# Moving about half of the shifted copies of the powers from VectorE to GpSimd in an attention-plus-MLP kernel

## The chip, the cores and the metric

The kernel runs on one core of a Trainium2 chip. A core has five engines that run side by side, each through its own instructions in a fixed order: TensorE (PE in the profile, its weight loads PEld), VectorE (DVE), ScalarE (ACT), GpSimd (POOL) and SyncE (SP, which here only issues transfers). They wait for one another through semaphores. The metric is the time of one execution on the device in microseconds, the median of several runs; lower is better.

## The reference, cut to what matters

The input x has 2048 rows of 640. Branch A is softmax attention with 32 heads of width 20, branch B a dense layer with the Mish activation; a sigmoid gate per row mixes them.

```python
def _A_ref(x, wqkv, wo):
    H = 32; Dh = D // H                                   # D = 640, Dh = 20
    qkv = (x @ wqkv).reshape(B, S, 3, H, Dh).transpose(2, 0, 3, 1, 4)
    scores = jnp.einsum("bhqd,bhkd->bhqk", q, k) * scale
    p = _softmax(scores, axis=-1)
    return jnp.einsum("bhqk,bhkd->bhqd", p, v).transpose(0, 2, 1, 3).reshape(B, S, D) @ wo

def _B_ref(x, w1, b1, w2):
    h = jnp.einsum("bsd,df->bsf", x, w1) + b1             # F = 1536
    sp = jnp.log1p(jnp.exp(-jnp.abs(h))) + jnp.where(h > 0, h, 0)
    return jnp.einsum("bsf,fd->bsd", h * jnp.tanh(sp), w2)

g = _sigmoid((x * gate_w).sum(-1, keepdims=True))
return g * a + (1 - g) * b
```

The costly part is attention: 32 heads with 2048 x 2048 scores each, every one of which needs an exponential.

## The kernel before, in words

**Tiling.** Four heads are worked on together, since a head is only 20 wide: they lie in the four 32-row strips of the PE array. With 8 sets of four heads and 4 blocks of 512 queries there are 32 groups, and each has 16 sets of 128 keys. A set of keys has four score rows (one for each head) of 128 x 512, each filling one bank of the accumulation memory. The score matmuls (`score`, line 1199) use the array by rows; the products of exponentials and values (`emit_pv`, line 1292) and all dense products (line 574) use it by columns, four side by side.

**Two ways to an exponential.** Most score rows go to ACT in pairs or threes (`emit_exp`, line 1249), into the ring of tiles E. The other sets of keys go to DVE. There a row is turned into a power of two by arithmetic alone (`power_of`, line 443): scores are scaled, an offset is added, and the result is written as a 16-bit integer whose bits, read as bf16, are about the power wanted. When all four rows of the set stand in a tile T (128 x 2048 in bf16), `d_shifts` (line 530) makes two more copies of it, in which the integer 43 or 86 is added to every element (line 538): the same powers, displaced by a fraction of an octave. PE multiplies the tile by the values (VA) and the two copies by scaled values (VD) and adds up all three, which averages out most of the error of the approximation. So a set on DVE takes four score rows from ACT, costs DVE four powers and two shifts, and costs PE three products instead of one.

**What sets the order.** Nothing is scheduled by the compiler. While the kernel is built, a loop (line 1728) steps through a modelled time, and asks at each step whether an engine that is free there has something to do: `step_pe`, `step_act`, `step_dve`, `step_pool`. Costs in the model are constants (a shift and a power 600 ns, the product on GpSimd 728). What is picked is emitted at once, so each engine's order is fixed in the built program; only the waits are left to the chip. Work for DVE stands in `dve_q` with a priority and a time from which it is ready, that for GpSimd in `pool_q`, first in, first out. The choices depend on some 27 numbers in `rule` (how many sets DVE may have open, when PE changes from scores to products, when it fills in dummy matmuls, line 1560, and so on), and `PLAN` (line 169) changes them at each of the 32 groups.

**Tiles of the DVE path.** Tiles for the powers come from `T_slots` (5 of them), tiles for the shifted copies from `U_slots` (4). A tile is free again when its readers are done: PE's products, and for the powers' tile both shifts too. `d_take` (line 416) opens a set only when a tile is free. A shift is issued only when the values' scaled copies are there and a U tile is free (`can`, line 546).

**GpSimd.** It does one product for each finished group (`normalise`, lines 1306 to 1382, `c` at line 1333): the attention output divided by the sum of the exponentials, on its way to the output projection. Before that it clears some tiles (lines 320, 334, 1429) and makes the identity matrix.

Of the kernel before, what the change touches and what calls it, by code (L numbers as in the profile page):

```python
# [14 lines left out]
I16 = mybir.dt.int16  # L15
F16 = mybir.dt.float16
PSUM = bass.MemoryType.PSUM
DEBUG = False
# [34 lines left out]
SEM = 70.0  # L53
# [5 lines left out]
DVE_TAIL = 100.0  # L59
# [4 lines left out]
def kernel(  # L64
# [12 lines left out]
    nc = tc.nc  # L77
    _, S, D = A_x.shape
# [6 lines left out]
    QC = 512  # L85
# [11 lines left out]
    SHIFT = (0, 43, 86)  # L97
# [7 lines left out]
    NSH = len(SHIFT) - 1  # L105
# [31 lines left out]
    RING = 18  # L137
    NST = 3
    NOT = 3

    rule = Rule()
    rule.LOW = 0.56
# [26 lines left out]
    PLAN = {  # L169
        0.0: {'AHEAD': 5000.0, 'BEHIND': 6000.0, 'D2': 1.0, 'DQ': 2, 'DQ3': 0, 'DQ4': 0, 'ETIGHT': 1, 'HEAT': 0.7, 'HROOM': 0.0, 'KEEP3': 2, 'LEAD': 5, 'LOW': 0.5, 'MARGIN': 0.0, 'MERGE': 0, 'NEAR': 99, 'NOPEN': 5, 'PAIR': 0, 'PVMAX': 3, 'Q3': 2, 'ROOM': 200.0, 'SWTH': 250.0, 'TWO': 9, 'VF': 0, 'VMIN': 2, 'WAIT1': -2000.0, 'WAIT2': 6000.0, 'WAITU': -200000.0},  # L170
        1.0: {'DQ3': 1, 'DQ4': 1, 'HEAT': 0.9, 'KEEP3': 1, 'LOW': 0.41, 'MARGIN': 30.0, 'NEAR': 5, 'PAIR': 2, 'PVMAX': 4, 'ROOM': 300.0, 'SWTH': 380.0, 'TWO': 2, 'VMIN': 1, 'WAIT2': 100000.0, 'WAITU': 0.0},
        2.0: {'DQ3': 0, 'HEAT': 0.7, 'HROOM': 100.0, 'LEAD': 4},
        3.0: {'AHEAD': 3000.0, 'DQ': 1, 'LEAD': 5, 'LOW': 0.5, 'MARGIN': 60.0, 'NEAR': 7, 'NOPEN': 4, 'ROOM': 100.0, 'VF': 2, 'WAIT1': 2000.0},
        4.0: {'DQ3': 1, 'DQ4': 3, 'LEAD': 4, 'NOPEN': 5},
        5.0: {'WAIT2': 6000.0},
        6.0: {'MARGIN': 150.0, 'NOPEN': 4, 'PAIR': 0, 'VMIN': 3, 'WAIT2': 100000.0},
        7.0: {'MARGIN': 100.0},
        8.0: {'AHEAD': 2000.0, 'DQ3': 3, 'DQ4': 2, 'HEAT': 0.8, 'KEEP3': 2, 'LEAD': 5},
        9.0: {'D2': 0.5, 'SWTH': 600.0, 'VMIN': 1},
        10.0: {'BEHIND': 2000.0, 'ETIGHT': 0, 'HEAT': 0.7, 'LOW': 0.6},  # L180
        11.0: {'KEEP3': 3, 'TWO': 1},
        12.0: {'HEAT': 0.8},
        13.0: {'BEHIND': 3000.0, 'NEAR': 9, 'Q3': 1},
        14.0: {'AHEAD': 5000.0, 'DQ3': 2, 'PAIR': 2, 'WAITU': 100000.0},
        15.0: {'BEHIND': 4000.0, 'DQ4': 0, 'KEEP3': 1, 'LOW': 0.41, 'MARGIN': 60.0, 'MERGE': 1, 'PAIR': 0, 'Q3': 3},
        16.0: {'ETIGHT': 1, 'LEAD': 6, 'WAIT2': 30000.0},
        17.0: {'KEEP3': 2},
        18.0: {'VMIN': 2, 'WAITU': 0.0},
        19.0: {'SWTH': 250.0},
        20.0: {'AHEAD': 2000.0, 'D2': 1.0, 'MERGE': 0, 'NOPEN': 5},  # L190
        21.0: {'DQ4': 1},
        22.0: {'LEAD': 5, 'WAIT2': 3000.0},
        23.0: {'D2': 0.5, 'HEAT': 0.7, 'LEAD': 6, 'VF': 1, 'WAIT2': 30000.0},
        24.0: {'MERGE': 1, 'VF': 2},
        25.0: {'VMIN': 1},
        26.0: {'DQ4': 2, 'NEAR': 12, 'Q3': 1},
        27.0: {'BEHIND': 3000.0, 'HEAT': 0.8, 'HROOM': 0.0, 'LOW': 0.44},
        28.0: {'ETIGHT': 0, 'MARGIN': 0.0},
        29.0: {'BEHIND': 6000.0, 'LOW': 0.38, 'NEAR': 9, 'WAIT2': 6000.0},
        30.0: {'DQ': 2, 'NOPEN': 4, 'Q3': 2, 'WAIT1': 0.0},  # L200
        31.0: {'DQ3': 3, 'LOW': 0.6, 'ROOM': 300.0, 'SWTH': 600.0, 'TWO': 9, 'VF': 0},
    }

    x2d = A_x[0]
# [92 lines left out]
    def load_x(c):  # L297
# [7 lines left out]
        out=wv0[:, :, 4 * DH : 4 * DH + 1], in_=gate_w.rearrange("(kt p o) -> p kt o", p=P, o=1)  # L305
# [38 lines left out]
    NG = len(groups)  # L344
    first, last = {}, {}
# [30 lines left out]
    U_slots = [Slot(f"T{i}") for i in range(NHOLD, NTS)]  # L376
# [65 lines left out]
    def power_of(dst, src):  # L442
        nc.vector.tensor_scalar(  # L443
            out=dst.bitcast(I16), in0=src,
            scalar1=inv_sqrt_dh * LOG2E * 128.0, scalar2=127.0 * 128.0 + BETA,
# [84 lines left out]
    def d_shifts(d, t):  # L530
        G, j = d["G"], d["j"]
        pv_items[G].append((t, j, (0, d["T"], d["slot"])))

        def shift(i, t):
            slot = t_slot(U_slots, t)
            slot.users = 4
            tile_ = work.tile([P, 4 * QC], BF16, tag=slot.tag, name="T")
            nc.vector.tensor_scalar(  # L538
                out=tile_[:, :].bitcast(I16), in0=d["T"][:, :].bitcast(I16),
                scalar1=float(SHIFT[i]), scalar2=None, op0=ALU.add,  # L540
            )
# [15 lines left out]


    def mm_pieces(n, fn, each):
# [594 lines left out]
    pv_items = [[] for _ in range(NG)]  # L1154
# [151 lines left out]
    def normalise(G, ready):  # L1306
        p, qc = groups[G]
        i = G % 2
# [92 lines left out]
    for k in range(NFILL):  # L1401
# [5 lines left out]
        out=wkp[:, :, :, DH:32], in_=w_top[:, :, :].rearrange("p k (h d) -> p k h d", h=4)  # L1407
# [17 lines left out]
    for p in range(NQ - NSB, NQ):  # L1425
        tag = "wqp" if p < NQ - 1 else f"wo{p}"
# [257 lines left out]
    def step_dve(t):  # L1684
        best = None
        for it in dve_q:
            if it[1] <= t and (it[6] is None or it[6](t)):
                due = it[1] + (WAIT0, rule.WAIT1, rule.WAIT2, MWAIT)[it[0]]
                if it[0] == 3:
                    due = min(due, it[7] + WAIT3)  # L1690
                if it[6] is not None and it[0] == 2 and cur["G"] > pv_G[0]:
                    due = min(due, it[1] + rule.WAITU)
                rank = (due, it[2])
                if best is None or rank < best[0]:
                    best = (rank, it)
# [32 lines left out]
    while pv_G[0] < NG or chains or chain[0] or dve_q or act_q or pool_q:  # L1728
# [23 lines left out]
        t = min([t + TICK] + [f for f in free.values() if f > t])  # L1752
# [73 lines left out]
```

## Time and profile before

| | |
|---|---|
| median of three runs | 726.15 us (725.95 to 728.13) |
| the profiled execution | 725.95 us |
| its span, first to last instruction | 724.2 us |
| TensorE's granted clock | 1.00 |
| DMA | 37.84 MB, mean 52 GB/s |

In the profile's rows, an instruction is named by line, engine and operation, with output<-input and their shapes, then how many there are, their busy time together in us, the mean of one in ns, and the idle time of the engine ahead of them with the engine that ended it. Instructions overlap on their engine: the next one starts before the last one's results are written, so the pace (start to start) is shorter than the duration of one. The list of waits gives who waited for whom, the total in us, how often, and the longest. The order of time gives the start, the length in us, and how many equal instructions were merged in the row. A table by stage has busy time and count for each engine in stretches of the span. The chain of work that ended last goes back from the last instruction to what released it, and so on to the start. On PE, ends are modelled, so a busy PE is not a PE at its peak.

### The profile page before, as it was taken

Reading aid. Unit: us, or ns where it says so; the run is one execution under the profiler, and the core shown is the slowest. Engines: PE = TensorE matmul, PEld = TensorE weight load, DVE = VectorE, ACT = ScalarE, POOL = GpSimd, SP = SyncE. Lnnn points to the kernel's source line nnn. Section 1 sums busy time; section 2 is a strip of 40 time slices with the busy share of each in tenths; the row PEclk is TensorE's granted clock in tenths of the full one; section 3 lists DMA queues with packets and bytes.
Section 4 is the critical chain, followed back from the end, with each engine's and each line's share of the span. In section 5 each row is a group of like instructions: output and inputs, shape, how many; then the busy total and the mean of one; then the engine's idle time right before and its main releaser. Section 6 shows DMA issues by size and latency. Waiting matters only on the chain.

```text
span 724.2 us, 24530 instructions
## 1 busy us (share of the span) xinstructions
PE 711.5 (98%) x10454; PEld 232.6 (32%) x10454; DVE 678.5 (94%) x1185; ACT 706.6 (98%) x726; POOL 32.7 (5%) x43
## 2 busy tenths in 40 slices
PE   7999999999999999999999999999999999999997
PEld 3433332333222433333332222222333333333332
DVE  4499999988999999999999999999999999999997
ACT  5899999999999999999999999999999999999996
POOL 2000000000000000000100000000000000000000
PEclk9999999999999999999999999999999999999999
DMA  9611222323221201111241232221202222232101
GB/s 246 180 24 34 50 45 43 68 42 93 45 41 32 64 15 15 25 34 37 43 90 42 48 77 43 77 47 29 42 7 44 57 37 48 38 47 44 34 28 37
DMA packets 123309, 37.84 MB, mean 52 GB/s; under 512 B 90880, under 2 KB 122640, under 8 KB 123200
## 3 DMA queue, kind: packets, MB, share of 16 engines
q1 hardware_dynamic: 121600, 35.76, 22.7%
q8 instruction: 81, 1.33, 0.8%
q10 hardware_dynamic: 1600, 0.53, 0.3%
q14 instruction: 28, 0.23, 0.1%
HBM read 22.29 MB, written 11.48 MB: 47 GB/s over the span
## 4 chain that ended last, share of the span: by engine, by line
PE 80%; ACT 11%; DVE 5%; issue 2%; DMA 1%; SPq 0%; DVEq 0%; ACTq 0%
PE Sp L1199 27%; PE Sp L574 26%; PE Sp L1292 24%; ACT E L1249 11%; PE Sp L1560 2%; DVE T L443 2%; DVE T L538 1%; DMA w_top<-in_A_wqkv_dram 1%; DVE big L1001 0%; PE Sp L1767 0%; ACT L1249 0%; PE Sp L1415 0%; DVE VA L762 0%; PE Sp L584 0%; DVE ot L1001 0%
## 5 line engine op out<-in xcount | busy, mean ns | idle before, releaser
L1249 ACT ACTIVATE E<-Sp 128x1024 bf16<-128x1024 f32 (+1 forms) x710 | 675.5, 1097 | 4.0 <-PE Sp L1199 3.4
L443 DVE TENSOR_SCALAR T<-Sp 128x512 int16<-128x512 f32 (+1 forms) x570 | 381.4, 696 | 16.1 <-PE Sp L1199 14.5
L1199 PE MATMUL Sp<-qT,kT 32*128 32x512 bf16 x2048 | 286.8, 384 | 4.9 <-ACT E L1249 1.8
L538 DVE TENSOR_SCALAR T<-T 128x2048 int16<-128x2048 int16 x292 | 196.4, 688 | 0.7 <-PE Sp L1292 0.2
L1199 PEld LDWEIGHTS <-kT 32*128 32x128 bf16 x2048 | 73.7, 91 | 267.9 <-issue 264.1
L1292 PE MATMUL Sp<-E,VA 128*21 128x512 bf16 x1464 | 139.6, 383 | 0.0
L1292 PE MATMUL Sp<-T,VD 128*21 128x512 bf16 x1168 | 109.3, 381 | 0.2 <-DVE T L538 0.2
L574 PE MATMUL Sp<-w_sb,big 128*32 128x320 bf16 x1536 | 78.7, 302 | 0.0
L574 PE MATMUL Sp<-xT,w1t 128*32 128x512 bf16 x960 | 74.4, 384 | 0.2 <-DVE big L828 0.2
L1292 PEld LDWEIGHTS <-VA 128*21 128x21 bf16 x2048 | 45.8, 90 | 65.1 <-issue 55.8
L1334 POOL TENSOR_TENSOR T<-T,rec 128x320 bf16<-128x320 f32 x31 | 27.5, 888 | 662.2 <-DVE rec L1327 606.9
L1292 PE MATMUL Sp<-T,VA 128*21 128x512 bf16 x584 | 56.4, 382 | 0.0
L574 PE MATMUL Sp<-xT,ws 128*32 128x512 bf16 x720 | 55.1, 383 | 0.3 <-DVE st L678 0.3
L574 PEld LDWEIGHTS <-big 128*32 128x32 bf16 x1536 | 33.4, 95 | 28.9 <-issue 20.8
L1292 PEld LDWEIGHTS <-VD 128*21 128x21 bf16 x1168 | 28.1, 90 | 28.3 <-issue 22.0
L828 DVE TENSOR_SCALAR big<-Sp,b1f 128x512 bf16<-128x512 f32 x48 | 35.6, 743 | 0.7 <-PE Sp L574 0.6
L574 PE MATMUL Sp<-wv,xT 128*32 128x81 bf16 (+2 forms) x960 | 32.8, 258 | 0.0
L574 PE MATMUL Sp<-wo_sb,od 128*32 128x320 bf16 (+1 forms) x608 | 32.2, 302 | 0.0
L574 PEld LDWEIGHTS <-w1t 128*32 128x32 bf16 x960 | 17.6, 94 | 28.0 <-issue 23.9
L678 DVE CAST st<-Sp 128x512 bf16<-128x512 f32 x36 | 24.4, 678 | 2.0 <-PE Sp L574 1.9
L1313 DVE STREAM_TRANSPOSE T<-Sp 128x512 f32<-128x512 f32 x32 | 22.7, 711 | 1.9 <-PE Sp L1292 1.8
L762 DVE CAST VA<-Sp 128x80 bf16<-128x80 f32 (+2 forms) x48 | 16.1, 373 | 7.5 <-PE Sp L574 7.3
(74 smaller groups left out, 205.1 us busy)
## 6 DMA issues: line engine op xcount, KB each, us to landing
w1t<-in_B_w_dram SPq DMA_DIRECT2D x24, 320.0 KB
q_dram<-st SPq DMA_DIRECT2D x20, 128.0 KB
out_dram<-ot SPq DMA_DIRECT2D x16, 160.0 KB
qT<-q_dram SPq DMA_DIRECT2D x124, 20.0 KB
o_dram<-T SPq DMA_DIRECT2D x120, 20.0 KB
kT<-k_dram SPq DMA_DIRECT2D x28, 80.0 KB
k_dram<-st SPq DMA_DIRECT2D x16, 128.0 KB
big<-in_A_x_dram SPq DMA_DIRECT2D x3, 640.0 KB
```

What stands on the lines that cost most here:

```text
L443: nc.vector.tensor_scalar(out=dst.bitcast(I16), in0=src, scalar1=inv_sqrt_dh * LOG2E * 128.0, scalar2=127.0 * 128.0 + BETA, op0=ALU.mult, ...
L538: nc.vector.tensor_scalar(out=tile_[:, :].bitcast(I16), in0=d["T"][:, :].bitcast(I16), scalar1=float(SHIFT[i]), scalar2=None, op0=ALU.add,)
L574: nc.tensor.matmul(out_[k : k + 32], lhsT=lhsT[:, k : k + 32], rhs=rhs, tile_position=(0, k), **kw)
L678: nc.vector.tensor_copy(out=res["st"][:, :], in_=ps[:, :])
L762: nc.vector.tensor_copy(out=VA[:, sts[i], h0 : h0 + nh, 0:DH], in_=ps[:, i, 0:n].rearrange("p (h d) -> p h d", d=DH),)
L828: nc.vector.tensor_scalar(out=big[:, slot.tag, (ft % 2) * QC : (ft % 2 + 1) * QC], in0=ps[:, :], scalar1=b1f[:, ft : ft + 1], scalar2=None ...
L1199: nc.tensor.matmul(ps_cols, lhsT=kT[p][32 * t_ : 32 * t_ + 32, j * P : (j + 1) * P], rhs=qT[G][32 * t_ : 32 * t_ + 32, :], tile_position=( ...
L1249: nc.scalar.activation(E[:, x : x + n, :], ps, ACT.Exp, scale=inv_sqrt_dh,)
L1292: nc.tensor.matmul(acc[32 * t_ : 32 * t_ + DH + 1, :], lhsT=lhsT, rhs=rhs, start=(pv_done[G] == 0), stop=(pv_done[G] == pv_total[G] - 1), ...
L1313: nc.vector.transpose(out=st["T1"][:, :, :].rearrange("p b r -> p (b r)"), in_=acc[:, :])
L1334: nc.gpsimd.tensor_tensor(out=T2[i][:, :].rearrange("p (b r) -> p b r", r=32)[:, :, 0:DH], in0=st["T1"][:, :, 0:DH], in1=st["rec"][:, :].u ...
L1560: nc.tensor.matmul(acc[32 * t_ : 32 * t_ + DH + 1, :], lhsT=zero_w[:, 0 : DH + 1], rhs=xT[:, 0, h0 : h0 + QC], start=False, stop=False, ti ...
```

## The change

Each shift of a finished set is now given to one of two engines (`choose_`). It goes to GpSimd if its number is not above `rule.PS` (0, 1 or 2), the group is not the last, and the work that stands in `pool_q` is under `rule.PB` (1500 to 6000 ns); otherwise it goes to DVE as before. PS is 0 up to group 2, then 1, from 6.5 on 2, and 0 again from 29.5 on.

On GpSimd the shift is a 32-bit integer addition: the tile of 16-bit integers is read as 1024 integers of 32 bits, and a constant that holds 43 or 86 in both halves is added (`step_t`, set at the start). It is done in four parts of 128 x 256, one for each head's row, so that PE can start with the first; each counts 640 ns in the model (`PCOST`). The powers' tile is given back when the fourth part is done.

The model also gets a rule for the two engines: a shift on DVE first waits until GpSimd's present instruction is over, and GpSimd starts nothing until that shift is done (`two_port`). The group's product goes to the head of `pool_q`. `PLAN` may now change the numbers at every half group, and all its values are other ones, so the order of all engines is a new one.

```diff
+    PCH = 4
+    PCOST = 640.0
+    PLAST = 1
...
+    rule.PS = 1
+    rule.PB = 3000.0
...
-        0.0: {'AHEAD': 5000.0, 'BEHIND': 6000.0, 'D2': 1.0, ...
-        1.0: {'DQ3': 1, 'DQ4': 1, 'HEAT': 0.9, ...
...
+        0.0: {... 'PB': 3000.0, 'PS': 0, 'PVMAX': 4, ...
+        0.5: {'DQ4': 1, 'NEAR': 9, 'WAIT2': 100000.0},
...
+        2.0: {'DQ4': 2, 'NEAR': 5, 'PS': 1, 'ROOM': 100.0, 'VMIN': 2, 'WAITU': 100000.0},
...
+        6.5: {'HEAT': 0.7, 'PS': 2},
...
+        29.5: {'DQ': 1, 'DQ4': 1, 'NOPEN': 2, 'PS': 0, 'Q3': 1, 'WAIT2': 100000.0},
...
+    step_t = consts.tile([P, NSH], I32, tag="step_t")
+    for i in range(NSH):
+        nc.gpsimd.memset(step_t[:, i : i + 1].bitcast(I16), SHIFT[i + 1])
...
+    two_port = [0.0]
...
+        def parts(i, t):
+            slot = t_slot(U_slots, t)
+            slot.users = 4
+            tile_ = work.tile([P, 4 * QC], BF16, tag=slot.tag, name="T")
+            n = 2 * QC // PCH
+            def part(k, t):
+                nc.gpsimd.tensor_tensor(
+                    out=tile_[:, :].bitcast(I32)[:, k * n : (k + 1) * n],
+                    in0=d["T"][:, :].bitcast(I32)[:, k * n : (k + 1) * n],
+                    in1=step_t[:, i - 1 : i].to_broadcast([P, n]), op=ALU.add,
+                )
+            def last(t):
+                d["slot"].users -= 1
+                d["slot"].free_at = max(d["slot"].free_at, t)
+                pv_items[G].append((t, j, (i, tile_, slot)))
+            for k in range(PCH):
+                pool_q.append((
+                    t, PCOST, (lambda t, k=k: part(k, t)), last if k == PCH - 1 else None, None
+                ))
+        def choose_(t, i):
+            if i <= rule.PS and G < NG - PLAST and sum(
+                x[1] if x[4] is None else PCH * PCOST for x in pool_q
+            ) < rule.PB:
+                pool_q.append((t, 0.0, (lambda t: parts(i, t)), None, can))
+                return
+            dve(
+                t, t, 600.0, (lambda t, i=i: shift(i, t)), prio=2, can=can,
+                done=lambda t, i=i: pv_items[G].append((t, j, (i,) + d["T%d" % i])),
+            )
...
         for i in range(1, NSH + 1):
-            dve(
-                t, t, 600.0, (lambda t, i=i: shift(i, t)), prio=2, can=can,
-                done=lambda t, i=i: pv_items[G].append((t, j, (i,) + d["T%d" % i])),
-            )
+            choose_(t, i)
...
-            dve(t, t, 140.0, b, prio=pr, done=lambda t: pool_q.append((t, 728.0, c, c_done)))
+            dve(t, t, 140.0, b, prio=pr, done=lambda t: pool_q.insert(0, (t, 728.0, c, c_done, None)))
...
+        if best[0] == 2 and best[6] is not None:
+            cost += max(free["POOL"] - t, 0.0)
+            two_port[0] = t + cost
...
     def step_pool(t):
-        if not pool_q or pool_q[0][0] > t:
-            return None
-        _, cost, fn, done = pool_q.pop(0)
-        fn(t)
-        done(t + cost + DVE_TAIL + SEM)
-        return cost
+        t0 = max(t, two_port[0])
+        for it in pool_q:
+            if it[0] <= t and (it[4] is None or it[4](t)):
+                pool_q.remove(it)
+                _, cost, fn, done, _ = it
+                fn(t0)
+                if done:
+                    done(t0 + cost + DVE_TAIL + SEM)
+                return t0 - t + cost
+        return None
```

More of the change, by code (lines that the diff above doesn't have):

```diff
@@ L15 @@
 I16 = mybir.dt.int16
+I32 = mybir.dt.int32
 F16 = mybir.dt.float16
@@ L169 @@
     PLAN = {
-        0.0: {'AHEAD': 5000.0, 'BEHIND': 6000.0, 'D2': 1.0, 'DQ': 2, 'DQ3': 0, 'DQ4': 0, 'ETIGHT': 1, 'HEAT': 0.7, 'HROOM': 0.0, 'KEEP3': 2, 'LEAD': 5, 'LOW': 0.5, 'MARGIN': 0.0, 'MERGE': 0, 'NEAR': 99, 'NOPEN': 5, 'PAIR': 0, 'PVMAX': 3, 'Q3': 2, 'ROOM': 200.0, 'SWTH': 250.0, 'TWO': 9, 'VF': 0, 'VMIN': 2, 'WAIT1': -2000.0, 'WAIT2': 6000.0, 'WAITU': -200000.0},
-        1.0: {'DQ3': 1, 'DQ4': 1, 'HEAT': 0.9, 'KEEP3': 1, 'LOW': 0.41, 'MARGIN': 30.0, 'NEAR': 5, 'PAIR': 2, 'PVMAX': 4, 'ROOM': 300.0, 'SWTH': 380.0, 'TWO': 2, 'VMIN': 1, 'WAIT2': 100000.0, 'WAITU': 0.0},
@@ L172 @@
[L172 to L201, printed above, removed]
+        0.0: {'AHEAD': 5000.0, 'BEHIND': 6000.0, 'D2': 1.0, 'DQ': 2, 'DQ3': 0, 'DQ4': 0, 'ETIGHT': 1, 'HEAT': 0.7, 'HROOM': 100.0, 'KEEP3': 3, 'LEAD': 5, 'LOW': 0.5, 'MARGIN': 0.0, 'MERGE': 0, 'NEAR': 99, 'NOPEN': 5, 'PAIR': 0, 'PB': 3000.0, 'PS': 0, 'PVMAX': 4, 'Q3': 3, 'ROOM': 200.0, 'SWTH': 250.0, 'TWO': 9, 'VF': 0, 'VMIN': 1, 'WAIT1': 0.0, 'WAIT2': 6000.0, 'WAITU': 0.0},
@@ new lines @@
+        0.5: {'DQ4': 1, 'NEAR': 9, 'WAIT2': 100000.0},
+        1.5: {'DQ3': 3, 'ETIGHT': 0, 'HEAT': 0.9, 'VMIN': 3},
+        2.0: {'DQ4': 2, 'NEAR': 5, 'PS': 1, 'ROOM': 100.0, 'VMIN': 2, 'WAITU': 100000.0},
+        2.5: {'AHEAD': 1000.0, 'Q3': 2},
+        3.5: {'AHEAD': 2000.0, 'NEAR': 7, 'Q3': 3, 'SWTH': 520.0, 'WAIT1': -2000.0},
+        4.0: {'MARGIN': 30.0, 'NEAR': 99, 'PVMAX': 2, 'VF': 2, 'VMIN': 1},
+        4.5: {'ETIGHT': 1, 'TWO': 2, 'VMIN': 3},
+        5.0: {'KEEP3': 1, 'LEAD': 4, 'LOW': 0.47, 'NOPEN': 4, 'Q3': 1, 'SWTH': 600.0, 'WAIT2': 3000.0},
@@ new lines @@
+        5.5: {'HROOM': -100.0, 'KEEP3': 3, 'LOW': 0.53, 'NEAR': 12, 'PVMAX': 3, 'VMIN': 2},
+        6.0: {'PVMAX': 2},
+        6.5: {'HEAT': 0.7, 'PS': 2},
+        7.0: {'DQ3': 2, 'NOPEN': 5, 'TWO': 9, 'VMIN': 1},
+        7.5: {'PB': 6000.0},
+        8.0: {'LEAD': 6, 'WAIT2': 30000.0},
+        8.5: {'HROOM': 100.0, 'MERGE': 1, 'NEAR': 9, 'Q3': 3, 'VF': 0, 'WAITU': -200000.0},
+        9.0: {'D2': 0.5, 'HEAT': 0.8, 'MERGE': 0, 'WAITU': 100000.0},
+        9.5: {'AHEAD': 3000.0, 'MERGE': 1, 'SWTH': 250.0, 'WAIT1': 0.0},
@@ new lines @@
+        10.0: {'PVMAX': 4, 'VF': 2},
+        10.5: {'HEAT': 0.9},
+        11.0: {'KEEP3': 1, 'ROOM': 300.0},
+        11.5: {'KEEP3': 2, 'ROOM': 100.0},
+        12.0: {'D2': 0, 'DQ': 1, 'LOW': 0.41, 'MERGE': 0, 'SWTH': 450.0},
+        12.5: {'NOPEN': 3, 'Q3': 1},
+        13.0: {'Q3': 3},
+        14.0: {'HROOM': -200.0, 'LOW': 0.47, 'WAIT2': 100000.0},
+        14.5: {'NOPEN': 2},
+        15.0: {'HEAT': 0.7},
+        15.5: {'HEAT': 0.9},
+        16.0: {'DQ3': 0, 'DQ4': 0, 'HROOM': -100.0},
@@ new lines @@
+        17.0: {'PB': 3000.0},
+        17.5: {'D2': 0.5, 'PB': 6000.0, 'TWO': 2},
+        18.0: {'ROOM': 200.0},
+        19.0: {'LOW': 0.6, 'NOPEN': 5},
+        19.5: {'DQ3': 2, 'DQ4': 3, 'ETIGHT': 0, 'KEEP3': 1, 'LOW': 0.53, 'TWO': 1},
+        20.0: {'DQ4': 1, 'MARGIN': 60.0, 'MERGE': 1, 'TWO': 2, 'WAIT1': -2000.0, 'WAITU': 0.0},
+        20.5: {'NEAR': 99, 'PB': 3000.0, 'SWTH': 380.0},
+        21.0: {'DQ4': 2, 'KEEP3': 3, 'NEAR': 7, 'PVMAX': 3},
+        21.5: {'ETIGHT': 1, 'MERGE': 0, 'PB': 6000.0, 'Q3': 2, 'WAIT2': 30000.0},
@@ new lines @@
+        22.0: {'HROOM': 0.0, 'ROOM': 100.0},
+        23.0: {'HROOM': -200.0, 'TWO': 1},
+        23.5: {'PVMAX': 2},
+        24.0: {'MARGIN': 30.0, 'NOPEN': 2, 'TWO': 9},
+        25.0: {'NOPEN': 4, 'PB': 1500.0, 'PVMAX': 4, 'ROOM': 200.0, 'SWTH': 520.0, 'WAIT2': 100000.0},
+        25.5: {'LEAD': 5, 'PB': 3000.0, 'WAIT2': 3000.0},
+        26.0: {'HROOM': 100.0, 'ROOM': 100.0, 'TWO': 2},
+        26.5: {'HROOM': -200.0, 'PVMAX': 2},
+        27.0: {'KEEP3': 2, 'WAIT1': 0.0, 'WAITU': 100000.0},
@@ L202 @@
+        27.5: {'LOW': 0.44, 'PVMAX': 4, 'Q3': 3},
+        28.0: {'DQ': 2, 'KEEP3': 3, 'MARGIN': 0.0},
+        28.5: {'LOW': 0.38, 'TWO': 9, 'WAIT2': 30000.0},
+        29.5: {'DQ': 1, 'DQ4': 1, 'NOPEN': 2, 'PS': 0, 'Q3': 1, 'WAIT2': 100000.0},
     }
```

## The prediction

> **What bounds the kernel now.** I read the page's engine totals first, then the table by stage (the columns are PE, PEld, DVE, ACT, POOL busy, granted clock, share of the DMA engines, GB/s).
>
> ```profile
> span 724.2 us, 24530 instructions
> PE 711.5 (98%) x10454; PEld 232.6 (32%) x10454; DVE 678.5 (94%) x1185; ACT 706.6 (98%) x726; POOL 32.7 (5%) x43
> ...
> 60.00:235.00 175.00, 174.28 (x2481) 53.08 (x2473) 165.51 (x285) 174.74 (x178) 7.46 (x9) 1.00 0.24 50
> 255.00:510.00 255.00, 254.41 (x3577) 75.83 (x3577) 252.13 (x427) 254.78 (x273) 10.68 (x12) 1.00 0.20 44
> 530.00:690.00 160.00, 159.47 (x2478) 54.48 (x2470) 155.34 (x266) 160.00 (x172) 7.67 (x8) 1.00 0.22 40
> 690.00:715.00 25.00, 25.00 (x381) 8.45 (x379) 24.83 (x46) 25.00 (x28) 0.73 (x1) 1.00 0.07 21
> ```
>
> Three engines are nearly full and one is empty. ACT stands out: in every stage between 60 and 715 us it is busy almost without a break, so the time there is the number of exponentials times their pace. The clock is 1.00 throughout and the DMA engines are mostly idle, so neither is in the argument. Which engine makes the others late is read from the chain of work that ended last, and from the list of waits:
>
> ```profile
> PE 80%; ACT 11%; DVE 5%; issue 2%; DMA 1%; SPq 0%; DVEq 0%; ACTq 0%
> ...
> ACT E L1249 <- PE Sp L1199: 3.4, 4, 2.1
> ...
> DVE T L443 <- PE Sp L1199: 14.5, 38, 1.0
> ```
>
> The chain goes through PE for 80%, yet ACT is seen idle for want of scores for only 3.4 us. Both hold at once because PE feeds ACT just in time. So I need ACT's stalls that hide inside "busy". The groups by line with shapes kept apart give them; the third row is the same view of 335.7 to 346 us alone, a stretch of two-bank exponentials only.
>
> ```profile
> L1249 ACT ACTIVATE E<-Sp 128x1024 bf16<-128x1024 f32 x666 | 622.4, 1072 | 3.5 <-PE Sp L1199 2.9
> L1249 ACT ACTIVATE E<-Sp 128x1536 bf16<-128x1536 f32 x44 | 65.5, 1490 | 0.5 <-PE Sp L1199 0.5
> ...
> L1249 ACT ACTIVATE E<-Sp 128x1024 bf16<-128x1024 f32 x13 | 12.0, 1087 | 0.0
> ...
> L1249 ACT ACTIVATE E<-Sp 128x1024 bf16<-128x1024 f32 (+1 forms) x710 | 675.5, 1097 | 4.0 <-PE Sp L1199 3.4
> ```
>
> In the undisturbed stretch 13 exponentials take 12.0 us; without the last one's full 1.09 us that is (12.0 - 1.09) / 12 = 0.909 us from start to start. A third bank adds 1.490 - 1.072 = 0.418 us. At that pace all of them would take 666 x 0.909 + 44 x 1.327 = 663.8 us; they took 675.5 busy and 4.0 idle. So ACT loses about **15.7 us** to late scores; the rest of the time is ACT's own work.
>
> **The change, part by part.** The counts after come from the two built programs, whose instructions can be counted without running them.
>
> 1. *ACT.* Before, 666 x 2 + 44 x 3 = 1464 score rows go through the exponential; after, 682 x 2 + 28 x 3 = 1448, in again 710 instructions. Sixteen rows (four sets of keys) go to DVE instead. At 0.418 us a row that is **-6.7 us** on the engine that sets the pace.
>
> 2. *PE.* The number of separate score rounds stays 721. The filler matmuls (line 1560) fall from 224 to 112, the products with powers rise from 3216 to 3248; four of them run side by side.
>
> ```profile
> L1292 PE MATMUL Sp<-E,VA 128*21 128x512 bf16 x1464 | 139.6, 383 | 0.0
> L1292 PE MATMUL Sp<-T,VD 128*21 128x512 bf16 x1168 | 109.3, 381 | 0.2 <-DVE T L538 0.2
> ...
> L1292 PE MATMUL Sp<-T,VA 128*21 128x512 bf16 x584 | 56.4, 382 | 0.0
> ...
> L1560 PE MATMUL Sp<-xT,zero_w 128*21 128x512 bf16 x224 | 20.9, 385 | 0.0
> ...
> 301.05 0.39 PE L1292 MATMUL Sp<-T,VA 128*21 128x512 bf16 x4
> ...
> 301.26 0.39 PE L1292 MATMUL Sp<-T,VD 128*21 128x512 bf16 x4
> ```
>
> The start times show 0.21 us for each four: (8 - 28) x 0.21 = -4.2 us. PE gets less to do, so it gives no reason for more stalls on ACT; I count the 4.2 us at nothing, since ACT's own work hides it.
>
> 3. *DVE.* Shifts on line 538 fall from 292 to 144; the power of a score row (line 443) is taken for 600 rows instead of 584 (2 x 14 + 556 before, 2 x 5 + 590 after).
>
> ```profile
> L443 DVE TENSOR_SCALAR T<-Sp 128x512 int16<-128x512 f32 x556 | 364.7, 683 | 16.0 <-PE Sp L1199 14.5
> L538 DVE TENSOR_SCALAR T<-T 128x2048 int16<-128x2048 int16 x292 | 196.4, 688 | 0.7 <-PE Sp L1292 0.2
> ...
> L443 DVE TENSOR_SCALAR T<-Sp 128x1024 int16<-128x1024 f32 x14 | 17.1, 1218 | 0.1
> ...
> 299.80 0.68 DVE L538 TENSOR_SCALAR T<-T 128x2048 int16<-128x2048 int16 x1
> ...
> 300.40 0.69 DVE L443 TENSOR_SCALAR T<-Sp 128x512 int16<-128x512 f32 x1
> ...
> 301.00 0.49 DVE L762 CAST VA<-Sp 128x320 bf16<-128x320 f32 x1
> ```
>
> Each costs 0.60 us from start to start. 148 x 0.60 = -88.8, 16 x 0.60 = +9.6, and about 0.6 for nine fewer paired powers: 678.5 becomes about 599.9 us before any new wait.
>
> 4. *GpSimd's work.* 624 additions of 128x256 in 32 bits, four for each of 156 shifts, 52% of all 300. The trace has no such instruction. The nearest rows are the product of line 1334 (128x320, also two inputs) and the select (128x128). The last two rows, of all products and of all shifts (least, median and longest ns; first and last start), give the products' total and the stretch in which shifts are wanted, 49 to 715 us.
>
> ```profile
> 132.97 0.73 POOL L1334 TENSOR_TENSOR T<-T,rec 128x320 bf16<-128x320 f32 x1 [17.97 <-DVE rec L1327]
> ...
> 1.07 0.29 POOL masks.py:199 TENSOR_SCALAR_AFFINE_SELECT ident<-ident 128x128 bf16<-128x128 bf16 x1
> ...
> L1334 POOL TENSOR_TENSOR T<-T,rec 128x320 bf16<-128x320 f32 x31 | 27.5, 888 | 662.2 <-DVE rec L1327 606.9 <-DMA kT<-k_dram 26.6 <-DVE rec L1329 14.5
> ...
> L538 DVE TENSOR_SCALAR T<-T x292: 629/684/1221, 49.1 to 714.8; 128x2048 int16<-128x2048 int16 x146
> ```
>
> By elements both give 0.58 us for 256 (0.73 x 256 / 320, 0.29 x 2); the whole product, 0.73 us, is the upper end. I take 0.60: 374 us, between 362 and 456, beside the 27.5 us of products. The order was written out with 640 ns for a part. GpSimd idles otherwise, so this costs nothing unless GpSimd falls behind.
>
> 5. *The new wait at the memory port.* The trace does show what happens when a shift and a GpSimd instruction meet:
>
> ```profile
> 74.62 1.77 DVE L538 TENSOR_SCALAR T<-T 128x2048 int16<-128x2048 int16 x2
> ...
> 74.85 0.98 POOL L1334 TENSOR_TENSOR T<-T,rec 128x320 bf16<-128x320 f32 x1 [14.13 <-DVE rec L1327]
> ...
> 309.11 1.28 DVE L538 TENSOR_SCALAR T<-T 128x2048 int16<-128x2048 int16 x2
> ```
>
> Two shifts alone take 1.28 us; with the product between them 1.77, and the product 0.98 for 0.73. Each waits for the other: the product lost 0.25 us to the first shift, the second shift 0.49 us to the product. So each of the 144 shifts left on DVE may wait between 0 and 0.49 us, 0 to 71 us in all. GpSimd is busy for (374 + 27.5) / 666 = 60% of that stretch and a shift comes on average midway, so I take 144 x 0.60 x 0.25 = 22 us. DVE then has 622 us of work (600 to 671), at each end less than the 678.5 it managed before. GpSimd waits too: at most 144 x 0.60 = 86 us, which makes 374 + 27.5 + 86 = 488 us (at most 570) of 666.
>
> In the Trainium skill, "SBUF — State Buffer", section "Who interferes with whom", says that a VectorE instruction in a two-port mode and a GpSimd instruction take the shared port pair in turn, for a whole instruction, and the second one is blocked. By that rule the trace agrees (0.49 and 0.25 us). "Perfetto Trace Analysis", section "Optimizing Scalar/DVE Operations", concludes that moving work from one to the other "might not help". That would hold if the shared port were the bound; by the sums above it is taken for about 488 us, and no run here yet shows parts back to back.
>
> 6. *What is queued behind the waits.* DVE works in order: behind a blocked shift stand the powers, which free score banks, so ACT starves if the block is long. In the order of the changed program, the shifted tiles that DVE makes are first used by PE a median of 3 score rounds after they were issued (2 before), a round being 724.2 / 721 = 1.0 us. GpSimd's tiles are used a median of 6 rounds after their last part, nine in ten of them 4 or more. A part that comes 1 us late delays no product there. New too: 55 powers and 31 shifts on DVE wait for GpSimd to have released a tile; that is in the rivals. Two small memsets of the step table stand ahead of the identity at the start; I count them at nothing, since PE then waits for x from memory, and at some 0.2 us if not.
>
> **The sum.** The profiled execution took 725.95 us, 1.75 more than its span and 0.2 less than the median of three, 726.15. Without the 6.7 us it is 719.3 us, if the stalls stay at 15.7. They can shrink, because PE and DVE have less to do, or grow, because waits at the port come irregularly. I choose a net 1.3 us off: **718 us**. The lower bound, with no stall left, is 719.3 - 15.7 = 703.6.
>
> **The rivals.**
>
> *A shift is passed over by a row of parts* (slower). The trace shows a shift waiting for one lone product. It does not show what happens when the next part is already queued at the port. If GpSimd keeps the port until its queue is empty, a shift waits for what is left of four parts, on average 2 x 0.60 = 1.2 us: 144 x 1.2 = 173 us, DVE at 773. It decides from (678.5 - 599.9) / 144 = 0.55 us for each shift, where DVE is as full as before. At 1.2 us the time would be about 773 + 45.7 (DVE's idle time now) + 1.75 = 820 us; at one part more than forecast, some 0.85 us, about 770. Against it: the two engines took turns in both directions above.
>
> *The tiles come free too late* (slower). A base tile is held until GpSimd has read its last part. GpSimd takes 4 x 0.60 = 2.4 us where DVE took 0.6, and the 55 powers wait in DVE's queue ahead of all others. If each waited 0.3 us that ACT does not hide, that is +16.5 us: 735. It decides from 55 x 0.12 = 6.7 us, the gain.
>
> *The gain is lost in jitter* (no change). Stalls rise from 15.7 to 22 us, 9 ns for each exponential: 726. For it speaks that ACT already waits for PE everywhere; against it, the lead of 3 and 6 rounds.
>
> *GpSimd becomes the bound* (slower). It would need parts over (666 - 27.5 - 86) / 624 = 0.89 us, well above both rows; at 1.0 us the work of 737 us from the first shift at 49 us on gives some 790 us.
>
> That the shifts do not move is excluded: the built program holds the 624 parts.
>
> **How the numbers follow.** Forecast, with stalls between none and 20 us (704 to 723.5): 0.75. Jitter, 724 to 728: 0.08. Tiles late, 728 to 745: 0.06. Passed over by a row of parts, 760 to 820: 0.09. GpSimd the bound: 0.02. A measurement of this kernel can tell about 0.3%, 2.2 us, from no change: faster (under 724.0) 0.75, the same 0.08, slower 0.17. The range runs from 706 (almost no stall left) to 736 (tiles a little late). Outside lie the two slow cases, half of the late tiles, and a little below: under 0.2.
>
> **What would show it.** ACT's exponentials: 682 and 28, busy about 669 us; if busy plus idle is above 679.5, the stalls ate the gain. DVE's total near 620 us; a shift's mean duration under 0.95 us (0.69 now) says one part's wait at most, over 1.3 us the first rival. A part on GpSimd at 0.58 to 0.73 us alone; its total under 570 us. In the list of waits, PE on GpSimd and DVE on GpSimd near zero; many us at the power's line would be the late tiles. The forecast is wrong if ACT's idle time grows at PE's scores, or if the rounds on PE lengthen although it has fewer matmuls.

## The result, and the profile after

The changed kernel takes 721.97 us (median of 6 runs, 721.37 to 722.66) against 725.91 us for the kernel before in the same series. The ratio is 0.9937, with a 95% interval of 0.9926 to 0.9948: 0.63% faster, 4.6 us by the ratio and 3.9 us by the medians. Forecast were 718 us and a range of 706 to 736.

The page of the changed kernel (its profiled execution took 721.37 us) has these totals and this chain:

```profile
span 719.5 us, 24904 instructions
...
PE 706.6 (98%) x10374; PEld 230.3 (32%) x10374; DVE 631.3 (88%) x1062; ACT 700.8 (97%) x726; POOL 417.7 (58%) x669
...
PE 86%; ACT 9%; issue 2%; DVE 1%; DMA 1%; SPq 0%; POOL 0%; DVEq 0%; ACTq 0%
```

DVE lost 47 us of work and GpSimd gained 385, but PE and ACT are as full as before. The page's groups say what became of ACT (its first row holds the two-bank and the three-bank exponentials together), and the second fence has the waits that matter:

```profile
L1312 ACT ACTIVATE E<-Sp 128x1024 bf16<-128x1024 f32 x710 | 669.5, 1074 | 4.9 <-PE Sp L1262 4.4
L572 POOL TENSOR_TENSOR T<-T,step_t 128x256 int32<-128x256 int32 x624 | 388.9, 657 | 107.5 <-PE Sp L1355 83.3
...
L604 DVE TENSOR_SCALAR T<-T 128x2048 int16<-128x2048 int16 x144 | 116.9, 817 | 1.5 <-PE Sp L1355 0.4
```

```profile
DVE T L473 <- PE Sp L1262: 44.8, 106, 1.3
...
ACT E L1312 <- PE Sp L1262: 4.4, 6, 1.8
...
DVE T L473 <- POOL T L572: 2.1, 4, 1.0
```

ACT's exponentials with their idle time went from 675.5 + 4.0 = 679.5 us to 669.5 + 4.9 = 674.4, 5.1 less; the span fell by 4.7. At the undisturbed pace of the prediction they would take 682 x 0.909 + 28 x 1.327 = 657.1 us, so 17.3 us are stalls, 1.6 more than before. The remaining 0.4 us is at the end: from the last exponential to the end of the span it is 8.7 us, 8.3 before. DVE now stands still for 44.8 us waiting for scores to take powers of (14.5 before): most of the time it was given is not used.

### The profile page after: what moved, and what is told of

Read it like the earlier page. It is cut to its first block, busy times and chain, and to the rows that moved or that the text cites. A ratio compares the mean times of both kernels' runs of the same rounds, so it can differ in the third digit from the quotient of the medians.

```text
span 719.5 us, 24904 instructions
## 1 busy us (share of the span) xinstructions
PE 706.6 (98%) x10374; PEld 230.3 (32%) x10374; DVE 631.3 (88%) x1062; ACT 700.8 (97%) x726; POOL 417.7 (58%) x669
## 4 chain that ended last, share of the span: by engine, by line
PE 86%; ACT 9%; issue 2%; DVE 1%; DMA 1%; SPq 0%; POOL 0%; DVEq 0%; ACTq 0%
PE Sp L1262 29%; PE Sp L637 28%; PE Sp L1355 27%; ACT E L1312 9%; PE Sp L1623 1%; DMA w_top<-in_A_wqkv_dram 1%; PE Sp L1837 0%; DVE T L473 0%; PE Sp L1478 0%; DVE T L604 0%; DMA qT<-q_dram 0%; POOL T L572 0%; DVE VD L424 0%; DVE ot L1861 0%; SPq L317 0%
## 5 line engine op out<-in xcount | busy, mean ns | idle before, releaser
L1312 ACT ACTIVATE E<-Sp 128x1024 bf16<-128x1024 f32 x710 | 669.5, 1074 | 4.9 <-PE Sp L1262 4.4
L572 POOL TENSOR_TENSOR T<-T,step_t 128x256 int32<-128x256 int32 x624 | 388.9, 657 | 107.5 <-PE Sp L1355 83.3
L473 DVE TENSOR_SCALAR T<-Sp 128x512 int16<-128x512 f32 (+1 forms) x595 | 392.0, 686 | 50.8 <-PE Sp L1262 44.8
L1397 POOL TENSOR_TENSOR T<-T,rec 128x320 bf16<-128x320 f32 x31 | 24.5, 790 | 164.8 <-DVE rec L1390 140.6
L604 DVE TENSOR_SCALAR T<-T 128x2048 int16<-128x2048 int16 x144 | 116.9, 817 | 1.5 <-PE Sp L1355 0.4
L1355 PE MATMUL Sp<-T,VD 128*21 128x512 bf16 x1200 | 113.2, 382 | 1.3 <-DVE T L604 1.3
L637 PE MATMUL Sp<-xT,w1t 128*32 128x512 bf16 x960 | 76.6, 383 | 0.0
L637 PEld LDWEIGHTS <-w1t 128*32 128x32 bf16 x960 | 19.6, 94 | 26.0 <-issue 20.9
```

Of the source, the lines that this page charges most:

```text
L473: nc.vector.tensor_scalar(out=dst.bitcast(I16), in0=src, scalar1=inv_sqrt_dh * LOG2E * 128.0, scalar2=127.0 * 128.0 + BETA, op0=ALU.mult, ...
L572: nc.gpsimd.tensor_tensor(out=tile_[:, :].bitcast(I32)[:, k * n : (k + 1) * n], in0=d["T"][:, :].bitcast(I32)[:, k * n : (k + 1) * n], in1 ...
L604: nc.vector.tensor_scalar(out=tile_[:, :].bitcast(I16), in0=d["T"][:, :].bitcast(I16), scalar1=float(SHIFT[i]), scalar2=None, op0=ALU.add,)
L637: nc.tensor.matmul(out_[k : k + 32], lhsT=lhsT[:, k : k + 32], rhs=rhs, tile_position=(0, k), **kw)
L1312: nc.scalar.activation(E[:, x : x + n, :], ps, ACT.Exp, scale=inv_sqrt_dh,)
L1355: nc.tensor.matmul(acc[32 * t_ : 32 * t_ + DH + 1, :], lhsT=lhsT, rhs=rhs, start=(pv_done[G] == 0), stop=(pv_done[G] == pv_total[G] - 1), ...
```

## The experiments

All times are medians; each ratio is to the kernel before, measured on the same chip (726.2 to 726.5 us). "The order" means that of the changed kernel, unless said otherwise.

| run | what it is | us | ratio (95%) |
|---|---|---|---|
| e1_one_part | a shift on GpSimd is one instruction | 746.78 | 1.028 (1.0267 to 1.0294) |
| e2_on_dve | the moved shifts go back to DVE, same order | 750.66 | 1.0334 (1.032 to 1.0348) |
| e3_tiny_parts | GpSimd's parts nearly empty | 725.52 | 0.9975 (0.9961 to 0.999) |
| e5_tiny_parts_late | the same, start-up mended | 719.16 | 0.9899 (0.9884 to 0.9914) |
| e6_five_parts | five parts for four | 729.25 | 1.0037 (1.0024 to 1.0049) |
| e4_rules_only | new rules, no shift on GpSimd, new order | 741.93 | 1.0215 (1.0199 to 1.023) |
| e8_gpsimd_old_rules | old rules, shifts on GpSimd, new order | 735.87 | 1.0144 (1.0119 to 1.0168) |
| e12_seven_more_exp | 7 exponentials done twice | 729.50 | 1.0051 (1.0033 to 1.0069) |
| e7_narrow_exp | exponentials over 448 of 512 columns | 720.86 | 0.9942 (0.9918 to 0.9966) |
| e9_before_no_filler | kernel before, its order, no fillers | 726.35 | 1.0 (0.9992 to 1.0009) |
| e10_after_no_filler | no fillers | 721.98 | 0.9949 (0.9935 to 0.9963) |
| e11_narrow_no_filler | 448 columns and no fillers | 718.13 | 0.9885 (0.9867 to 0.9902) |

### Is it GpSimd's share, or the new rules?

**e2_on_dve** puts the shifts back without touching the order:

```diff
-                nc.gpsimd.tensor_tensor(out=..., in0=..., in1=step_t..., op=ALU.add)   # each part
+                if k == 0:
+                    nc.vector.tensor_scalar(out=tile_..., in0=d["T"]..., scalar1=float(SHIFT[i]), op0=ALU.add)
```

> The order is that of the changed kernel, but the 156 shifts of GpSimd are done by DVE, each at the place of its first part. Theory (the order is possible only because GpSimd carries the shifts): DVE has 631 - 18.6 + 156 x 0.60 = 706 us of work, more than the 678.5 us of before, and powers stand behind the added shifts: 728 to 745 us. Rival (the gain comes from the new rules and from fewer rows on ACT, who does the shifts matters little): 720 to 724 us.

Measured: 750.66 us, 29 us above the changed kernel, some 6 us beyond the theory's range. Its page's totals and chain, and its two-bank exponentials from the groups with shapes kept apart:

```profile
PE 729.9 (98%) x10374; PEld 234.6 (31%) x10374; DVE 692.6 (93%) x1218; ACT 713.5 (95%) x726; POOL 30.8 (4%) x45
...
PE 61%; DVE 28%; ACT 3%; DMA 3%; issue 2%; SPq 2%; ACTq 0%; DVEq 0%
```

```profile
L1312 ACT ACTIVATE E<-Sp 128x1024 bf16<-128x1024 f32 x682 | 647.3, 1033 | 21.1 <-PE Sp L1262 15.2 <-ACT E L1312 0.2
```

DVE is not even full; it is late, and the chain of work that ended last now goes through it for 28% (1% in the changed kernel). The extra shifts stand ahead of powers, the powers free the banks, PE's scores come late and ACT idles for 21.1 us, where the changed kernel showed 4.9. In this order the move is what carries the time.

**e4_rules_only** and **e8_gpsimd_old_rules** let the order be worked out anew with one half of the change each:

```diff
-    rule.PS = 1            # and every 'PS' in PLAN
+    rule.PS = 0
```

```diff
     PLAN = {               # the rows of the kernel before, with
+        0.0: {'PS': 0, 'PB': 3000.0, ...}, 2.0: {'PS': 1, ...}, 6.0: {'PS': 2, 'PB': 6000.0, ...}, 29.0: {'PS': 0, ...}
```

> The new rules at every half group, but all shifts on DVE (no shift may go to GpSimd); the order is worked out anew: 147 sets on DVE, 294 shifts, 328 filler matmuls. Theory (GpSimd's share is what makes room): ACT has 1460 rows, 12 more than in the changed kernel, and DVE is as full as before (about 680 us): 724 to 733 us. Rival (the finer rules alone bring the gain): 720 to 723 us.

> The rules of the kernel before (one set for each group), with shifts allowed to GpSimd in the same groups as in the changed kernel: 158 shifts on GpSimd, 136 on DVE, 147 sets, 216 filler matmuls. Theory (the gain is in the rows taken from ACT, and these rules take only four rows, 1460 for 1464): 722 to 728 us. Rival (room on DVE alone brings the gain, whatever the rules): 716 to 721 us. Second rival (rules chosen for another order break it): 732 us or more.

Both are slower than the kernel before, by 2.2% and 1.4%, and both beyond what the theory allowed (in e8 the second rival had it). The rules were chosen for one particular order; why they choose badly here no run shows. The lists of waits point at single places for a part of the loss: in e4, ACT stands idle three times, for 11.3 us in all, behind PE's products; in e8, the last output waits for PE for 8.8 us (3.6 in the changed kernel).

```profile
ACT E L1312 <- PE Sp L1355: 11.3, 3, 7.2
```

```profile
ACT ot L1832 <- PE Sp L1817: 8.8, 1, 8.8
```

So neither half, with its numbers left as they are, brings the gain alone. These two runs say nothing finer: each is one order among many, and neither half was given rules chosen for it.

### What the port and GpSimd's time cost

**e3_tiny_parts** and **e5_tiny_parts_late** leave most of each shifted copy out, so that GpSimd hardly works:

```diff
-                    out=tile_[:, :].bitcast(I32)[:, k * n : (k + 1) * n], ...  in1=....to_broadcast([P, n])
+                    out=tile_[:, :].bitcast(I32)[:, k * n : k * n + 2], ...    in1=....to_broadcast([P, 2])
+    # shifted tiles in fixed places, cleared once on GpSimd: first thing (e3), after the start-up work (e5)
```

> The order is that of the changed kernel, the shifted tiles lie in fixed places, and each part on GpSimd adds only the first two integers of its row instead of 256, so that most of the shifted copy is left out. GpSimd's time and the waits at the port nearly vanish: shifts on DVE back to 0.69 us each, DVE about 612 us. Theory (ACT sets the pace, DVE's waits are hidden by its idle time): 720 to 722 us. Rival (the 1.6 us of added stalls and more come from the port): 714 to 719 us.

> As the kernel with tiny parts (each part adds only two integers of its row, most of the shifted copy is left out), but the fixed tiles are cleared on GpSimd only after the start-up work that the first exponentials wait for. Theory (the 725.5 us there came from the start, where TensorE's clock fell to 0.5 for 10 us while GpSimd cleared tiles, and the waits at the port are hidden): 719.5 to 722 us, at most 2.5 us less than the changed kernel. Rival (the fixed tiles themselves, or short parts, make the order slower): 724 us or more again. Second rival (the port gave back the gain): 717 us or less.

e3 missed both ranges. Its page shows where the time went: GpSimd clears tiles in the first slice, the clock falls there, and the first exponential starts at 18.0 us instead of 10.7.

```profile
PE   6999999999999999999999999999999999999997
...
POOL 6000221112222121222122122222321122220000
PEclk7999999999999999999999999999999999999999
```

e5 clears them later and takes 719.16 us, 2.8 us less than the changed kernel (by the two ratios 2.8 +- 1.3 us; the spans of the two profiled executions differ by 1.3). That is just under the theory's range, so the waits are not wholly hidden, and above that of the second rival. Here are DVE's total and the exponentials on e5's page, and then the shift on DVE, first in e5, then in the changed kernel (the view of one line: least, median and longest ns, first and last start):

```profile
PE 706.6 (98%) x10374; PEld 230.8 (32%) x10374; DVE 613.4 (85%) x1062; ACT 699.3 (97%) x726; POOL 145.3 (20%) x673
...
L1313 ACT ACTIVATE E<-Sp 128x1024 bf16<-128x1024 f32 x710 | 668.1, 1079 | 5.0 <-PE Sp L1263 4.7
```

```profile
L605 DVE TENSOR_SCALAR T<-T x144: 628/684/846, 44.8 to 704.3; 128x2048 int16<-128x2048 int16 x144
```

```profile
L604 DVE TENSOR_SCALAR T<-T x144: 623/694/2195, 44.5 to 705.5; 128x2048 int16<-128x2048 int16 x144
```

Waiting for GpSimd costs DVE 144 x (0.817 - 0.688) = 18.6 us; 62 of the 144 shifts took over 0.75 us. DVE has more idle time than that, yet some 2.8 us reach the end. The likely way is that a wait falls on the powers queued behind it, and it shows at ACT: the exponentials with their idle time take 668.1 + 5.0 = 673.1 us in e5, 1.3 less than in the changed kernel. The run takes away GpSimd's own time together with the waits, so how the 2.8 us divide between the two is open.

**e1_one_part** makes the wait longer without changing the order:

```diff
-            for k in range(PCH): part(k)                          # 4 x 128x256
+            part 0 alone: tensor_tensor over [P, PCH * n]         # 1 x 128x1024
```

> The order of all engines is that of the changed kernel, but each shift on GpSimd is one instruction of 128x1024 instead of four of 128x256. Theory (ACT sets the pace; the waits at the port cost little because they are short against the lead of the tiles and because DVE has idle time): a shift on DVE now waits for up to 2.3 us, on average 0.6 x 1.15 = 0.7 us where it waited 0.13 us; 144 x 0.57 = 82 us more on DVE, 631 + 82 = 713 us, more than the 678.5 us it managed before, so the time rises to 727 to 742 us. Rival (the waits are hidden by the lead whatever their length): 721 to 723.5 us.

Measured: 746.78 us, above the theory's range. GpSimd has even less to do in sum, yet the shifts on DVE rise to 1.02 us on average. The last two rows are the view of the shift's line and the wait of ACT:

```profile
L573 POOL TENSOR_TENSOR T<-T,step_t 128x1024 int32<-128x1024 int32 x156 | 303.1, 1957 | 221.0 <-PE Sp L1355 107.5 <-DVE T L473 92.1 <-PE Sp L1262 14.6
...
L604 DVE TENSOR_SCALAR T<-T 128x2048 int16<-128x2048 int16 x144 | 146.6, 1023 | 1.6 <-PE Sp L1355 0.4
...
L604 DVE TENSOR_SCALAR T<-T x144: 632/690/2415, 44.6 to 732.2; 128x2048 int16<-128x2048 int16 x144
...
ACT E L1312 <- PE Sp L1262: 24.0, 37, 3.2
```

```profile
PE 719.2 (96%) x10374; PEld 232.5 (31%) x10374; DVE 661.5 (89%) x1062; ACT 706.3 (95%) x726; POOL 332.6 (45%) x201
```

The expectation had put the cost into DVE's total (713 us); that total is only 661.5. What costs are single long waits: most shifts take 0.69 us as before, the longest 2.4, and ACT idled 24.0 us for scores (4.4 in the changed kernel). Late tiles are not the reason: in this run's list, PE never waits for GpSimd, and DVE once, for 1.0 us. In this order, the four parts are what makes the move worth while.

**e6_five_parts** does the first part twice:

```diff
-                nc.gpsimd.tensor_tensor(...)
+                for _ in range(2 if k < 1 else 1): nc.gpsimd.tensor_tensor(...)
```

> The changed kernel with its first part of every shift done twice, so five parts of 0.57 us instead of four: 780 x 0.57 = 445 us on GpSimd, with products and waits some 515 of the 584 us in which it has shifts to do. Theory (tiles of GpSimd are used 6 us after their last part, so a lateness of 0.6 to 2 us is hidden; the waits at the port grow by a quarter, some 5 us, hidden too): 721 to 725 us. Rival (tiles that come free late and jitter decide): 729 us or more.

Measured: 729.25 us, 7.3 us above the changed kernel; the rival's side. The chain of its page now goes through GpSimd for 15%, and PE, which never waited for GpSimd in the changed kernel, does so 8 times:

```profile
PE 69%; POOL 15%; ACT 8%; DVE 4%; issue 2%; DMA 0%; SPq 0%; DVEq 0%; POOLq 0%; ACTq 0%
...
PE Sp L1356 <- POOL T L573: 1.9, 8, 0.6
```

GpSimd's lead of 6 rounds does not carry a quarter more work, although between its first and its last part it is busy for 513 of 594 us, so not all of the time. That the lateness adds up where several shifts stand in its queue is the likely reason; it was not traced.

### Which engine sets the pace?

**e12_seven_more_exp** gives ACT back about what the change took from it:

```diff
+        n_exp[0] += 1
-            nc.scalar.activation(E[:, x : x + n, :], ps, ACT.Exp, scale=inv_sqrt_dh)
+        for _ in range(2 if n_exp[0] % 100 == 50 else 1):
+            nc.scalar.activation(E[:, x : x + n, :], ps, ACT.Exp, scale=inv_sqrt_dh)
```

> The changed kernel with 7 of its 710 exponentials done twice, spread over the span: ACT gets 7 x 0.909 = 6.4 us more, as much as the change took from it (6.7 us); nothing else is changed. Theory (ACT has no slack, so its rows are the gain): 727 to 730 us, the kernel before or a little above. Rival (PE sets the time and ACT catches up): 721.5 to 724 us.

Measured: 729.50 us, 7.5 us more for 6.4 us of work. ACT has no slack to catch up with.

**e7_narrow_exp** goes the other way; it leaves out part of the attention (448 of 512 queries of a block get exponentials):

```diff
-            E[:, x : x + n, :], ps, ACT.Exp, scale=inv_sqrt_dh,
+            E[:, x : x + n, 0:NE], ps[:, :, 0:NE], ACT.Exp, scale=inv_sqrt_dh,       # NE = 448
```

> The order of the changed kernel, but each exponential covers 448 of the 512 columns of its banks (the other columns of the ring stay at one, so part of the attention is left out). ACT is relieved of 1448 x 64 x 0.82 ns = 76 us of 670. Theory (ACT alone sets the pace): time falls by 50 to 76 us, to 646 to 672 us. Rival (PE stands right behind ACT, 721 score rounds with two changes of tiling each): time falls by less than 25 us, to 697 us or more.

Measured: 720.86 us, only 1.1 us less than the changed kernel; by the ratios (0.9942 and 0.9937) there is no difference at all. The theory that ACT alone sets the pace falls in this direction. Here is the longest stage of the table by stage (columns as in the prediction's first fence), first in e7, then in the changed kernel, and then e7's exponentials, waits and chain:

```profile
255.00:510.00 255.00, 254.80 (x3576) 75.34 (x3572) 237.00 (x381) 242.60 (x273) 185.14 (x294) 1.00 0.21 45
...
255.00:510.00 255.00, 254.78 (x3572) 75.84 (x3564) 236.57 (x380) 254.32 (x273) 184.78 (x294) 1.00 0.21 45
```

```profile
L1314 ACT ACTIVATE E<-Sp 128x896 bf16<-128x896 f32 x710 | 637.3, 932 | 36.5 <-PE Sp L1264 26.2
...
ACT E L1314 <- PE Sp L1264: 26.2, 112, 2.1
...
PE 90%; DMA 3%; SPq 2%; DVE 2%; POOL 1%; ACT 1%; issue 0%; ACTq 0%; DVEq 0%; POOLq 0%
```

PE is as full as before, so its busy time tells nothing here. But ACT now waits for it 112 times (6 in the changed kernel), the chain goes through PE for 90%, and the exponentials with their idle time take 637.3 + 36.5 = 673.8 us, hardly less than the 674.4 of the changed kernel: ACT's own work shrank, and waiting took its place. That suggested a new theory, PE alone, and **e9** and **e10** took PE's fillers away:

```diff
-            for t_ in range(4):
-                nc.tensor.matmul(acc[32 * t_ : 32 * t_ + DH + 1, :], lhsT=zero_w..., rhs=xT..., ...)
```

> The kernel before, in its own order, without its 224 filler matmuls (56 groups of four, they add zeros). New theory (PE sets the pace: its groups follow each other at full pace, and the change gained what it took from PE): 56 x 0.21 = 12 us less, 713 to 716 us. First theory (ACT sets the pace, PE waits for it in the places of the fillers): 725 to 727 us. Third (the fillers keep TensorE's clock up): the granted clock falls and the time is above 727 us.

> The changed kernel, in its own order, without its 112 filler matmuls (28 groups of four). PE sets the pace: 28 x 0.21 = 5.9 us less, 715 to 717 us. ACT sets the pace, or PE waits in the fillers' places anyway: 721 to 723 us. If the fillers keep the clock up: the granted clock falls and the time is above 723 us.

No difference in either order: 726.35 and 721.98 us. So the new theory fell as well; the fillers seem to stand where PE waits for ACT anyway. What fits all four runs (e7, e9, e10, e12) is that both engines are full, each in its own places. **e11_narrow_no_filler** (both edits) tests that:

> The changed kernel with exponentials over 448 of 512 columns (part of the attention is left out) and without its 112 filler matmuls. Theory (ACT and PE are both full, and the fillers only fill the places in which PE waits for ACT): with ACT relieved, PE alone sets the time, and the 28 groups of fillers now count: 720.9 - 5.9 = 715 us, 713 to 717.5 us. Rival (something else sets the time, the banks or DVE's order): 719.5 to 722 us again.

Measured: 718.13 us, 2.7 us below e7 (by the two ratios 4.1 +- 2.2 us), between the two ranges. With ACT relieved the fillers do begin to cost, about half of their 5.9 us or somewhat more. That a second limit stands right behind ACT is shown, and that PE is at least a part of it; the banks or DVE's order are not excluded as the rest.

## Why the prediction was right, point by point

The direction, the range and the size of the main term held; the forecast was 4 us too low, because the stalls grew where the prediction let them shrink (point 5).

1. *ACT, -6.7 us.* Confirmed as the source of the gain: the counts and the 669 us of busy time are as forecast, and adding 6.4 us to ACT gave 7.5 us back (e12). No run takes the sixteen rows from ACT in the old order, so what they would be worth without the rest of the change is open.
2. *PE's 4.2 us at nothing.* Confirmed for the fillers by e9 and e10: taken away from either kernel, they change nothing. But the prediction's **lower bound of 703.6 us was wrong**: it let ACT lose all its stalls and did not ask how fast PE can go. In this order the kernel takes 718 to 721 us even when ACT is relieved of 76 us (e11, e7).
3. *DVE, 622 us.* It has 631.3, 9 more, and the waits for GpSimd are not the reason: without them e5 still has 613.4 us where the prediction counted 599.9. It took shifts and powers at 0.60 us from start to start, but one that starts behind an idle gap takes its whole 0.69. DVE waits for scores 106 times now against 38, which makes 68 x 0.09 = 6 us by estimate; the rest is open. As forecast DVE is no longer tight. What that room is worth by itself no run shows; in this order it is needed (e2).
4. *GpSimd.* A part takes 0.610 us (median) and 0.57 from start to start, against 0.60 estimated; 389 us against 374, waits in it.
5. *The port.* 22 us of waits were forecast for DVE, 18.6 measured. That they lie so close is partly luck: 60% of the shifts were to wait 0.25 us each, and 62 of 144 (43%) took longer, by some 0.31 us each. The prediction spread GpSimd's work over 666 us, but with PS = 0 at both ends its parts run from 66 to 651 us only, and 35 of the 144 shifts lie outside. The mistake is the next step, in which the waits were **hidden** by DVE's idle time: some 2.8 us come through (e5, with GpSimd's own time). With them the sum is 719.3 + 2.8 = 722.1 us, beside 721.97 measured; with +- 1.3 us on the 2.8, that agreement is luck too. The "net 1.3 us off" for shrinking stalls had the wrong sign: ACT's stalls grew by 1.6 us, and in e5 they are back at 673.1 - 657.1 = 16.0, near the 15.7 of before. One of the signs that the prediction named for being wrong, more idle time of ACT at PE's scores, did show in small (4.4 us against 3.4).
6. *The lead of 3 and 6 rounds.* Enough as it stands (DVE waits for GpSimd's release 2.1 us in 4 times), but not a reserve: one more part per shift cost 7.3 us (e6).

The rivals. *Passed over by a row of parts*: it happens to one shift of 144, near 524 us, which lasted through three parts:

```profile
522.74 3.45 POOL L572 TENSOR_TENSOR T<-T,step_t 128x256 int32<-128x256 int32 x6
```

```profile
524.55 2.19 DVE L604 TENSOR_SCALAR T<-T 128x2048 int16<-128x2048 int16 x1
```

The rows are GpSimd's and DVE's in order of time. All other shifts lasted under 1.2 us, so they waited for no more than the part in progress. The rival's price (820 us, or 770) also let every shift meet a part, where 62 did. *Jitter* came true for a quarter (1.6 of 6.7 us). *Tiles too late* and *GpSimd the bound* did not happen, but the threshold of the second was too generous: e6's work is 5 x 0.61 / 4 = 0.76 us for each of four parts, under the 0.89 us of the prediction, and GpSimd is on the chain already. The 0.89 came from the stretch of 666 us; over the 585 us in which the parts run it is (585 - 27.5 - 86) / 624 = 0.76 us, where e6 stands.

The rule of the Trainium skill that was weighed ("SBUF — State Buffer", "Who interferes with whom") holds here too: in e1 the shift waits for the rest of an instruction of 1.89 us, the longest takes 2.4 us, and the mean rises from 0.82 to 1.02 us. The warning of the Trainium skill's "Perfetto Trace Analysis" ("Optimizing Scalar/DVE Operations") that moving work between the two engines might not help comes true in a small part only: in this fixed order the move is worth 29 us (e2), with some 2.8 us that GpSimd's work costs (e5) already taken off.

## What to carry to other kernels

When an engine is full, ask at once how full the next one is: taking 76 us from ACT here was worth 1 us at most, because a second limit, at least in part PE, stood right behind it. That bounds the gain that less work on ACT can bring in this order. A wait on an engine with idle time is not free when the instructions queued behind it feed the bottleneck; cut the work that is waited for into short instructions (four parts 722 us, one part 747). Rules tuned for one order are a part of that order: with its numbers left as they are, neither half of this change worked without the other.

## What the runs showed of the hardware

GpSimd's 32-bit addition takes a median of 0.196, 0.610 and 1.892 us for 2, 256 and 1024 integers in each partition (e5, the changed kernel, e1):

```profile
L573 POOL TENSOR_TENSOR T<-T,step_t x624: 188/196/758, 66.3 to 646.5; 128x2 int32<-128x2 int32 x156
```

```profile
L572 POOL TENSOR_TENSOR T<-T,step_t x624: 602/610/1157, 66.0 to 650.1; 128x256 int32<-128x256 int32 x156
```

```profile
L573 POOL TENSOR_TENSOR T<-T,step_t x156: 1883/1892/2432, 66.1 to 674.8; 128x1024 int32<-128x1024 int32 x156
```

That is (1892 - 610) / 768 = 1.67 ns for each integer, and six parts in a row take 3.45 us, (3.45 - 0.61) / 5 = 0.57 us from start to start. "GPSIMD Engine Reference" of the Trainium skill (section "Performance versus the Vector engine") gives 2.6 cycles an element for two inputs and counts with 1.2 GHz, which makes an estimate of 2.2 ns. The runs show less, here with a second input that is one broadcast value; whether that is the reason no run shows.

Without its fillers the kernel before ran at about half the clock for some 10 us, around the end of the Mish activation on ACT, and still took the same time (first e9, then the kernel before):

```profile
517.00:528.00 11.00, 10.84 (x86) 2.69 (x88) 8.15 (x15) 9.94 (x6) 0.00 (x0) 0.53 0.00 0
...
517.00:528.00 11.00, 10.78 (x149) 3.66 (x145) 9.70 (x17) 10.97 (x6) 0.00 (x0) 1.00 0.01 1
```

With the fillers the clock stays at 1.00 there, but in these runs that is worth nothing (726.35 us without, 726.34 with). In the profiled execution of e10, the granted clock is 0.95 from 60 to 510 us, and it took 727.95 us where the median is 721.98; what lowered the clock no run shows.
